# Filler matmuls in a fused attention and MoE kernel: one PSUM tile for a run of them instead of one each

## The chip, the cores and the metric

The kernel runs on one core of a Trainium2 chip. The metric is the device time of one execution in microseconds (us). Three runs of the kernel before gave 780.67, 783.67 and 1508.87 us, and their median is 783.67 us.

## The reference

Three layers follow each other. The first is an attention with a memory of 32 slots per head; its result is turned into 2304 rows of 512 numbers. The second and third are feed-forward layers on these rows. In short:

```
a      = softmax(phi, over the 32 slots)              # 4 batches, 8 heads, 576 positions
k_m    = a^T k ; v_m = a^T v                          # 32 x 64 per head
attn   = softmax(q k_m^T / 8) v_m                     # 576 x 64 per head
x      = rows of attn                                 # 2304 x 512
xn     = x / rms(x) * rms_g
h      = silu(xn @ w_gate) * (xn @ w_val)             # 2304 x 1536
x2     = h @ w_out                                    # 2304 x 512
h2     = x2 @ w_in                                    # 2304 x 2048
g      = h2 where h2 >= 1, 0 where h2 <= -1, else (h2 + 1)^2 / 4
result = g @ w_out2                                   # 2304 x 512
```

## The kernel before, in words

The kernel is one long list of instructions without loops on the chip. A planner (the class `Agenda`) runs while the program is built. Each piece of work is a stream, written as a Python generator; a stream tells the planner which engine it wants next and for how long, and the planner lets the stream with the earliest start go on. The instructions stand on each engine in the order in which the planner released them, and the engines keep that order.

The attention comes first. `soft(b)` (from line 524) takes batch b's `phi`: VectorE folds a maximum `pm` (L516), TensorE transposes it into the PSUM tile `mps` (L534), VectorE reduces it to `gm` (L539), TensorE spreads `gm` again over the partitions (L545, four matmuls), VectorE subtracts it from `phi` (L553) and ScalarE takes the exponential (L521). `memory(b)` (L603, 144 matmuls named `kvps`) then multiplies it with `k` and `v`, and L622 adds the sums. `pair(n)` makes queries (L769), scores (L720) and the attention's output (L841). Beside it the weights of the second layer come in through the buffers `raw`, are converted by ScalarE and VectorE (lines 339 to 362) and go on to the stage of `gps` and `vps` (L981). After that come `ops` (L1076), the seven products of `w_in` (L1420) and those of `w_out2` (L1543).

All loads but two are issued by SyncE's queue, in the planner's order. The first batch of loads brings `phi`, `k`, `v` of two batches and one `q`; a third `phi` follows when the first `phi`'s buffer comes free, which is after L622 of batch 0.

The change is in `heat()` (from line 578). It issues matmuls of a tile of zeros, 128x512, into a PSUM bank that nothing reads. They stand where the planner had TensorE idle, until the memory of the fourth batch is done (`HEAT`, line 40, flag `('km', 3)`). The planner books 0.2133 us for one, and picks a free bank `z` for it. Every other PSUM tile comes from the same pool, one buffer for each of the eight banks; a bank that a stream gives back is noted with its time in `agenda.given[z]`. A new tile of a pool in a buffer that an older tile held has to wait for the last user of the older tile. That wait is a semaphore on the first instruction that writes the new tile, and it is put there also where the last user was TensorE itself.

Of the kernel before, what the change touches and what calls it, by code (L numbers as in the profile page):

```python
# [9 lines left out]
F32 = mybir.dt.float32  # L10
# [6 lines left out]
P = 128  # L17
# [212 lines left out]
def tile_attn_moe(tc, q, k, v, phi, w_gate, w_val, w_out1, rms_g, w_in2, w_out2, out):  # L230
# [46 lines left out]
    psum = top.enter_context(tc.tile_pool(name="psum", bufs=1, space=bass.MemoryType.PSUM))  # L277
# [28 lines left out]
    agenda = Agenda({**BUFS, "th": 0, "xs": 0, "ab": 0, "gs": 0, "wo": 0, **{("bank", z): 1 for z in range(8)}})  # L306
# [270 lines left out]

    def heat():

        while HEAT[0] not in agenda.flags:  # L580
            z = yield "heat", 0.2133
            t = psum.tile([P, 512], F32, tag=f"b{z}", name="heat")
            nc.tensor.matmul(  # L583
                out=t.rearrange("p (x n) -> p x n", x=2), lhsT=zeros[:, 0:P],
                rhs=zeros.unsqueeze(1).to_broadcast([P, 2, 256]), start=True, stop=True,
                skip_group_check=True,
            )
# [625 lines left out]
    if HEAT:  # L1213
        add(10**6, heat())
# [451 lines left out]
```

## Time and profile before

| what | value |
|---|---|
| median of three runs | 783.67 us |
| the profiled execution | 782.0 us |
| its span | 780.2 us |
| TensorE busy in the span | 768.4 us |
| VectorE busy | 621.8 us |
| ScalarE busy | 462.9 us |
| GpSimd busy | 61.1 us |
| data moved by DMA | 197.49 MB, mean 253 GB/s |
| heat matmuls | 46, the first at 1.0 us, the last at 85.5 us |

The span runs from the first to the last instruction that the profile counts; 1.8 us of the execution lie around it. Busy time is the time in which an engine had an instruction in work; a matmul counts from its start to its modelled end, so matmuls that are pipelined overlap in it. "PE" is TensorE's matmuls, "PEld" its weight loads, DVE is VectorE, ACT ScalarE, POOL GpSimd, SP SyncE. The chain of waits is followed back from the last instruction: from each instruction to what released it, or to the one before it on its engine.

### The profile page before, as it was taken

The numbers are of one execution on the slowest core, as the hardware profiler recorded it, in microseconds if no ns is written. First come the engines' busy times: TensorE is split into PE (matmuls) and PEld (weight loads), VectorE is DVE, ScalarE is ACT, GpSimd is POOL, SyncE is SP. The second block draws the span as 40 slices with busy tenths as digits, with TensorE's granted clock in tenths as the row PEclk, the third lists the DMA queues.
The fourth block names the chain that finished last, engine by engine and source line by source line (L and its number), as shares of the span: only waits on it lengthen the run. The fifth ranks groups of instructions, "written<-read, shape, count | busy, mean of one in ns | idle before, by whom it ended". The sixth has DMA issues, their size and how long they took to land.

```text
span 780.2 us, 17231 instructions
## 1 busy us (share of the span) xinstructions
PE 768.4 (98%) x6383; PEld 701.0 (90%) x6383; DVE 621.8 (80%) x1257; ACT 462.9 (59%) x959; POOL 61.1 (8%) x84
## 2 busy tenths in 40 slices
PE   8999999999999999999999999999999999999997
PEld 1777788889989888988889999999999999999997
DVE  2798979999878787756688989997779895689963
ACT  1488877765566654656566656564457464565452
POOL 1266710000000000000000000000000000000000
PEclk9999999999999999999999999999999999999999
DMA  9984546587878765599746999779878978857876
GB/s 341 327 319 150 197 170 209 204 272 262 281 248 286 249 243 199 191 324 311 250 161 208 310 310 295 259 246 321 291 241 267 304 231 260 259 184 245 276 225 199
DMA packets 113371, 197.49 MB, mean 253 GB/s; under 512 B 10372, under 2 KB 41096, under 8 KB 113288
## 3 DMA queue, kind: packets, MB, share of 16 engines
q1 hardware_dynamic: 112368, 194.88, 75.1%
q10 hardware_dynamic: 920, 1.51, 0.5%
q8 instruction: 51, 0.84, 0.4%
q14 instruction: 32, 0.26, 0.1%
HBM read 151.26 MB, written 45.09 MB: 252 GB/s over the span
## 4 chain that ended last, share of the span: by engine, by line
PE 94%; DVE 2%; ACT 1%; issue 1%; DMA 1%; SPq 0%; DVEq 0%; ACTq 0%
PE ops L1076 18%; PE acc_b L1543 16%; PE qb L1420 12%; PE gps L981 10%; PE vps L981 10%; PE qc L1420 6%; PE acc_c L1543 6%; PE qa L1420 3%; PE vwps L931 3%; PE heat L583 3%; PE xp L841 2%; PE kvps L603 1%; PE sc L720 1%; PE qps L769 1%; DMA x1B<-x_d 1%
## 5 line engine op out<-in xcount | busy, mean ns | idle before, releaser
L1076 PE MATMUL ops<-ab,wo1h 128*128 128x512 f32 (+1 forms) x480 | 137.2, 371 | 0.5 <-ACT xs L1090 0.5
L1420 PE MATMUL qb<-xop,wr 128*128 128x384 f32 x576 | 111.9, 338 | 0.0
L1420 PEld LDWEIGHTS qb<-xop,wr 128*128 128x128 f32 x576 | 100.5, 187 | 0.9 <-DVE xop L1295 0.5
L1076 PEld LDWEIGHTS ops<-ab,wo1h 128*128 128x128 f32 x480 | 84.6, 189 | 15.8 <-issue 2.9
L1076 PE MATMUL ops<-ab,wo1l 128*128 128x512 f32 (+1 forms) x240 | 88.4, 368 | 0.0
L1543 PE MATMUL acc_b<-wor,gg_A 128*128 128x256 f32 x648 | 80.8, 280 | 1.0 <-ACT gg_A L1491 0.8
L1543 PEld LDWEIGHTS acc_b<-wor,gg_A 128*128 128x128 f32 x648 | 79.3, 188 | 1.3 <-ACT gg_A L1491 1.0
L1382 ACT ACTIVATE u<-qb 128x384 f32<-128x384 f32 x72 | 35.2, 490 | 50.0 <-PE qb L1420 49.4
L1420 PE MATMUL qc<-xop,wr 128*128 128x384 f32 x288 | 58.4, 337 | 0.0
L1543 PE MATMUL acc_c<-wor,gg_S 128*128 128x256 f32 x432 | 53.0, 279 | 0.0
L1076 PEld LDWEIGHTS ops<-ab,wo1l 128*128 128x128 f32 x240 | 45.3, 189 | 7.9
L1543 PEld LDWEIGHTS acc_c<-wor,gg_S 128*128 128x128 f32 x432 | 52.2, 188 | 0.0
L1543 PE MATMUL acc_b<-wor,gg_S 128*128 128x256 f32 x432 | 51.7, 279 | 0.0
L1543 PEld LDWEIGHTS acc_b<-wor,gg_S 128*128 128x128 f32 x432 | 51.3, 188 | 0.0
L1420 PEld LDWEIGHTS qc<-xop,wr 128*128 128x128 f32 x288 | 51.0, 187 | 0.0
L344 ACT ACTIVATE raw<-raw 128x512 uint32<-128x512 uint32 x68 | 45.4, 674 | 0.0
L1013 ACT ACTIVATE kvth<-gps 128x64 f32<-128x64 f32 (+2 forms) x101 | 28.9, 305 | 18.4 <-PE gps L981 18.2
L981 PE MATMUL gps<-late,vwh 128*128 128x288 f32 x192 | 39.6, 294 | 0.0
L981 PE MATMUL vps<-late,vwh 128*128 128x288 f32 x192 | 39.6, 294 | 0.0
L951 DVE TENSOR_TENSOR vwl<-vwps,vwh 128x512 fp32r<-128x512 f32 x48 | 32.3, 684 | 7.2 <-ACT vwh L949 6.9
L1047 ACT ACTIVATE ab<-kvth 128x512 fp32r<-128x512 f32 (+1 forms) x40 | 22.7, 567 | 24.8 <-PE ops L1076 24.8
L1491 ACT ACTIVATE gg_S<-gs 128x384 fp32r<-128x384 f32 x52 | 26.8, 522 | 17.5 <-PE acc_b L1543 8.5
(188 smaller groups left out, 1739.8 us busy)
## 6 DMA issues: line engine op xcount, KB each, us to landing
wr<-win_d SPq DMA_DIRECT2D x168, 256.0 KB, 3.9
wor<-wout_d SPq DMA_DIRECT2D x168, 256.0 KB, 3.4
raw<-in_moe_w_out_dram SPq DMA_DIRECT2D x28, 512.0 KB, 4.7
win_d<-wins SPq DMA_DIRECT2D x56, 256.0 KB, 3.3
wout_d<-wouts SPq DMA_DIRECT2D x56, 256.0 KB, 3.2
raw<-in_moe_w_in_dram SPq DMA_DIRECT2D x16, 512.0 KB, 5.1
raw<-in_moe_w_gate_dram SPq DMA_DIRECT2D x12, 512.0 KB, 4.8
raw<-in_moe_w_val_dram SPq DMA_DIRECT2D x12, 512.0 KB, 5.5
```

The lines of the kernel that those rows point to most:

```text
L344: nc.scalar.activation(out=low, in_=low, func=AF.Copy, scale=LOW_SCALE, bias=LOW_BIAS)
L583: nc.tensor.matmul(out=t.rearrange("p (x n) -> p x n", x=2), lhsT=zeros[:, 0:P], rhs=zeros.unsqueeze(1).to_broadcast([P, 2, 256]), start=T ...
L931: nc.tensor.matmul(out=vps[g][0][32 * c : 32 * c + 32, 2 * P * x : 2 * P * x + 2 * P], lhsT=vT[n // NF1 * 2 + x][hs, c, :], rhs=t[hs, c].r ...
L951: nc.vector.tensor_tensor(out=lv, in0=vps[g][0], in1=hv.bitcast(F32), op=ALU.subtract)
L981: nc.tensor.matmul(out=p[:, 0:HB], lhsT=wt[:, g, i, :], rhs=at[b][:, g, c], start=(g == 0 and y == 0), stop=(g == 1 and y == 2),)
L1013: nc.scalar.activation(out=t, in_=g[:, c], func=AF.Silu)
L1047: nc.scalar.activation(out=ah, in_=src, func=AF.Copy)
L1076: nc.tensor.matmul(out=p[:, 0:n], lhsT=wt[:, fc, d], rhs=at, start=(fc == 0 and x == 0), stop=(fc == NF1 - 1 and x == 2),)
L1382: nc.scalar.activation(out=u, in_=src, func=AF.Copy)
L1420: nc.tensor.matmul(out=bank, lhsT=wt[:, kc, :], rhs=xt[:, kc, :], start=(start and kc == 0 and i == 0), stop=(kc == 1 and i == 2), skip_gr ...
L1491: nc.scalar.activation(out=t[:, 0], in_=src, func=AF.Copy)
L1543: nc.tensor.matmul(out=acc[x + "001"[t]][:, t % 2], lhsT=g[:, gi, P * t : P * t + P], rhs=w[:, wi], start=((o, t) in FIRST and q == 0 and ...
```

## The change

A run of heat matmuls keeps its PSUM tile as long as the planner names the same bank for the next one and no stream has given that bank back in between. Otherwise it takes a new tile, as before.

```diff
     def heat():
 
+        last = t = None
         while HEAT[0] not in agenda.flags:
             z = yield "heat", 0.2133
-            t = psum.tile([P, 512], F32, tag=f"b{z}", name="heat")
+            if last != (z, agenda.given.get(z)):
+                last = z, agenda.given.get(z)
+                t = psum.tile([P, 512], F32, tag=f"b{z}", name="heat")
             nc.tensor.matmul(
```

No engine's instructions change their order, and none is added or taken away; all lines after 579 are numbered three higher. What changes are semaphore waits on TensorE: of the 46 heat matmuls, 41 lose a wait on TensorE's own semaphore, and 5 other matmuls get one.

TensorE's first instructions, before the change (`zeros` is the tile of zeros, `heat` the bank's tile, the waits stand in brackets, and a wait on TensorE itself reads PE_49):

```order
L583 LDWEIGHTS zeros [waits DVE_49]
L583 MATMUL heat<-zeros 128x512
L583 LDWEIGHTS zeros
L583 MATMUL heat<-zeros 128x512 [waits PE_49]
...
L534 MATMUL mps_174<-ident,pm_155 128x128 [waits DVE_49,Pool_49]
```

The same place in the changed program:

```order
L586 LDWEIGHTS zeros [waits DVE_49]
L586 MATMUL heat<-zeros 128x512
L586 LDWEIGHTS zeros
L586 MATMUL heat<-zeros 128x512
...
L534 MATMUL mps_155<-ident,pm_142 128x128 [waits DVE_49,Pool_49]
```

In both, 21 heat matmuls stand ahead of the transpose into `mps`; before, the second to the twenty-first wait for the one ahead of them, and after, none of them waits.

TensorE at the transpose of batch 1, before the change:

```order
L583 LDWEIGHTS zeros
L583 MATMUL heat<-zeros 128x512 [waits PE_49]
L534 MATMUL mps_322<-ident,pm_258 128x128 [waits DVE_49]
L769 MATMUL qps_0_0_324<-ident,q_203 128x128 [waits DMAHW5_49]
L769 MATMUL qps_0_0_324<-ident,q_203 128x128 x3
L657 MATMUL kT_334<-ident,kd_302 128x128
```

The same place in the changed program:

```order
L586 LDWEIGHTS zeros
L586 MATMUL heat<-zeros 128x512
L534 MATMUL mps_287<-ident,pm_229 128x128 [waits DVE_49,PE_49]
L772 MATMUL qps_0_0_289<-ident,q_176 128x128 [waits DMAHW5_49]
L772 MATMUL qps_0_0_289<-ident,q_176 128x128 x3
L660 MATMUL kT_299<-ident,kd_273 128x128
```

Here the wait has moved from the heat matmul to the transpose behind it. The other four matmuls that get such a wait are three first matmuls of a `qps` (L769 before, L772 after) and the first of an `aTp` (L820, L823).

## Rows read from the trace of the kernel before

**Rows 1.** The page: shares of the chain of waits by line.

```profile
PE ops L1076 18%; PE acc_b L1543 16%; PE qb L1420 12%; PE gps L981 10%; PE vps L981 10%; PE qc L1420 6%; PE acc_c L1543 6%; PE qa L1420 3%; PE vwps L931 3%; PE heat L583 3%; PE xp L841 2%; PE kvps L603 1%; PE sc L720 1%; PE qps L769 1%; DMA x1B<-x_d 1%
```

**Rows 2.** Stretches: us; PE, PEld, DVE, ACT, POOL busy (instructions); granted clock, DMA share, GB/s.

```profile
20.00:25.00 5.00, 4.72 (x144) 3.03 (x128) 3.37 (x16) 0.00 (x0) 0.61 (x1) 1.00 0.53 168
25.00:30.00 5.00, 4.84 (x59) 3.40 (x58) 3.02 (x5) 4.32 (x8) 1.30 (x2) 1.00 1.05 404
...
40.00:60.00 20.00, 18.58 (x387) 15.05 (x391) 18.76 (x40) 17.67 (x37) 14.08 (x16) 1.00 0.89 318
...
100.00:200.00 100.00, 100.00 (x896) 88.92 (x895) 88.60 (x191) 68.72 (x160) 2.79 (x2) 1.00 0.67 225
...
400.00:780.00 380.00, 374.32 (x2665) 372.42 (x2663) 308.83 (x601) 211.56 (x416) 0.00 (x0) 1.00 0.80 259
```

**Rows 3.** TensorE in order of time: start, us, line, operation, tiles, count.

```profile
1.04 13.41 PE L583 MATMUL heat<-zeros 128*128 128x512 bf16 x21 [1.04 <-DVE zeros L435]
14.24 0.42 PE L534 MATMUL mps<-ident,pm 128*128 128x128 f32 x1
...
16.28 3.13 PE L583 MATMUL heat<-zeros 128*128 128x512 bf16 x7
...
19.50 2.25 PE L603 MATMUL kvps<-kv,phi 64*32 64x128 f32 x144
...
22.00 2.55 PE L583 MATMUL heat<-zeros 128*128 128x512 bf16 x6
24.38 0.27 PE L534 MATMUL mps<-ident,pm 128*128 128x128 f32 x1
```

**Rows 4.** The chain of waits in order of time: start, us, what.

```profile
13.22 0.60 PE heat L583
...
16.88 0.39 PE heat L583
17.31 0.39 PE heat L583
...
44.05 1.27 issue
```

**Rows 5.** TensorE in the stage of L981, in order of time.

```profile
180.00 0.29 PE L981 MATMUL vps<-Al,vwh 128*128 128x288 f32 x1
180.13 0.29 PE L981 MATMUL vps<-Ah,vwl 128*128 128x288 f32 x1
```

**Rows 6.** VectorE in order of time: start, us, line, operation, idle ahead.

```profile
6.43 0.29 DVE L516 TENSOR_TENSOR pm<-pm,phi 128x128 f32<-128x128 f32 x1
...
16.40 1.42 DVE L553 TENSOR_TENSOR phi<-phi,mps 128x576 f32<-128x576 f32 x2 [1.41 <-PE mps L545]
...
23.29 0.28 DVE L516 TENSOR_TENSOR pm<-pm,phi 128x128 f32<-128x128 f32 x1
...
24.69 0.29 DVE L539 TENSOR_REDUCE gm<-mps 128x2 f32<-128x128 f32 x1 [0.79 <-PE mps L534]
...
25.83 1.35 DVE L553 TENSOR_TENSOR phi<-phi,mps 128x1152 f32<-128x1152 f32 x1 [0.52 <-PE mps L545]
...
42.02 1.18 DVE L341 TENSOR_SCALAR w<-raw 128x512 f32<-128x512 f32 x1
43.90 0.69 DVE L807 TENSOR_REDUCE sm<-e 128x16 f32<-128x512 f32 x1 [0.70 <-ACT e L803]
```

**Rows 7.** ScalarE in order of time: a load's issue, and the first exponential.

```profile
1.33 0.42 ACTq L465 DMA_DIRECT2D kv<-in_k_dram  x1
...
17.19 1.35 ACT L521 ACTIVATE phi<-phi 128x576 f32<-128x576 f32 x2 [10.94 <-DVE phi L553]
```

**Rows 8.** SyncE in order of time: the first gate weights' issue.

```profile
24.21 1.43 SPq L326 DMA_DIRECT2D raw<-in_moe_w_gate_dram  x1
```

**Rows 9.** Loads issued at 1.33 and at 24.21: queue, count, KB, us to landing.

```profile
kv<-in_k_dram ACTq DMA_DIRECT2D x1, 1152.0 KB, 10.0
...
raw<-in_moe_w_gate_dram SPq DMA_DIRECT2D x1, 512.0 KB, 13.3
```

## The prediction

> **What bounds the kernel now.** I read the page's chain of waits first, then stretches of the span, then each engine in order of time where the edited matmuls stand, and last the loads.
>
> The chain is TensorE nearly everywhere, and the heat matmuls, which compute nothing, are 3% of it [rows 1]. The stretches show why their place matters. From 100 us on TensorE has no gap (100.00 of 100 us; 374.32 of the last 380), so whatever brings it to 100 us earlier should end the kernel earlier by as much [rows 2]. Between 40 and 60 us TensorE (18.58 of 20), VectorE (18.76) and ScalarE (17.67) are all nearly full [rows 2].
>
> In order of time TensorE begins with 21 heat matmuls, from 1.04 to about 14.2 us, and only then comes the first real one, the transpose into `mps` at 14.24 [rows 3]. Its operand `pm` was ready on VectorE at 6.43 + 0.29 = 6.72 us [rows 6]. So the start of the kernel waits 7.5 us for filler: it has become the bound there.
>
> Why the filler is so slow shows in its records. A heat takes 0.60 us early on, and 21 of them from 1.04 to 14.45 are one per 0.64 us; from 16.88 on each takes 0.39 and starts 0.43 after the one ahead [rows 3, 4]. Each starts only when the one ahead is over, which is what a wait on TensorE itself makes. Matmuls without such a wait run closer than they last: at 180 us those of 288 columns start 0.13 apart and last 0.29, both into one bank [rows 5].
>
> **The clock.** The granted clock reads 1.00 in every stretch [rows 2], so I take the level from durations. [...] The heats of 0.60 us ran at the lower level until after 13.22, those from 16.88 on at the upper; between them stand `mps` and the heats behind it.
>
> **The change, step by step.** No instruction moves; 41 heats lose their wait and five other matmuls get one.
>
> 1. *The first 21 heats.* They now follow each other. Bounds: all at the lower level, 1.04 + 21 x 0.43 = 10.07 us; all at the upper, 1.04 + 21 x 0.22 = 5.66, but then the transpose waits for `pm`, 6.8. The clock starts low and rose in the trace once the work came closer, so I take half of them at each level: 1.04 + 10.5 x 0.43 + 10.5 x 0.22 = 7.9. Against 14.24 that is 6.4 earlier.
> 2. *From the transpose to VectorE's subtraction.* It took 16.40 - 14.24 = 2.16 us [rows 3, 6], with two waiting heats and the lower clock in it. In batch 1 the same way took 25.83 - 24.38 = 1.45, with foreign work in it, and its first leg 24.69 - 24.38 = 0.31; with `gm`'s 0.29 the least is 0.6. I take 1.2, nearer to the whole second round. The subtraction and the exponential end 17.19 + 1.35 - 16.40 = 2.14 later [rows 6, 7], unchanged. The exponential is done at 7.9 + 1.2 + 2.1 = 11.2 instead of 18.54.
> 3. *The next seven heats* delayed `kvps` to 19.50, 0.96 us after its exponential. Seven at 0.22 are 1.5 us beside 2.1 us of VectorE and ScalarE, so they vanish behind these. Now `k` is late next: issued at 1.33, landed 10.0 later, 11.33 [rows 7, 9]. `kvps` starts at about 11.4: **8.1 us earlier**. With step 1 at its slow end it would be 10.07 + 2.16 + 2.14 = 14.4, 5.1 earlier.
> 4. *Six heats at 22.00* end with the second transpose at 24.38, while its `pm` was ready at 23.29 + 0.28 = 23.57 [rows 3, 6]. Six at 0.22 are 1.3 instead of 2.55, so `pm` is what it waits for: another **0.75**.
> 5. *The other ten heats* would save up to 0.21 each, 2.1 in all. I count nothing: VectorE and ScalarE, nearly full there [rows 2], are late next. Bounds 0 to 2.1.
> 6. *Five new waits* sit on matmuls that follow heats in a bank. [...]
> 7. *What gives back: the loads.* They can't all come 8.85 us earlier. The DMA share is 0.53 from 20 to 25 us and 1.05 in the 5 us behind it [rows 2]: half of 5 us, 2.5, is empty, because the queue waits for `phi`'s buffer, and that hole closes. The first gate weights, landed at 24.21 + 13.3 = 37.5 [rows 8, 9], land at 35.0 at best. VectorE uses them at 42.02, which would now be 33.2, so it waits 1.8; 0.7 of that it idled anyway ahead of L807 [rows 6]. **Back: 1.1.** Bounds 0 (absorbed in the buffers) and the whole excess over the hole, 8.85 - 2.5 = 6.35.
>
> Sum: -8.1 - 0.75 + 1.1 = -7.75. Against the profiled execution's 782.0 us (span 780.2 and 1.8 around it) that is **774.3 us**. The median, 783.67, is 1.7 above that execution, and the nearer two of the three runs, 780.67 and 783.67, lie on both sides of it, so I use no other base.
>
> **The rivals.**
>
> *The loads become the bound.* From 25 us on the queues are full (1.05) [rows 2]. If everything up to 60 us hangs on them, only the hole's 2.5 us come through, and the end is 782.0 - 2.5 = 779.5. For it: the full queues, and three engines that are nearly full together. Against it: the gate weights landed 4.5 us ahead of their use. Anything between this and the forecast is possible too. Chance 0.25.
>
> *The change frees the wait but not the pace.* The waits are gone from the program, but if a run of writes into one bank can't come closer, nothing changes: 782. Against it stand the two matmuls in one bank at 0.13 us [rows 5]. With all other ways in which the shift could be lost before 100 us: chance 0.1.
>
> *More comes through.* The weights' delay is absorbed and the ten other heats count: 782.0 - 8.85 - 2.1 = 771.1. Chance 0.07.
>
> *Slower: the clock falls.* Shorter heats leave longer gaps ahead of `kvps` and the scores. In the trace TensorE ran at the lower level for the 13 us in which it waited after every heat [rows 3, 4]. If it falls back after the first heats and stays low to 60 us, about half of its busy time there (0.21 of the 0.39 of a heat) doubles: some 20 of its 40 us, 782.0 - 8 + 20 = 794. It becomes slower than before if it stays low for over 16 us of busy time. Against it: the same columns now stand closer together, and in the trace the clock held from 17 us on with wider spacing. [...] No row here shows a fall after 16.88, so I keep the chance at 0.06.
>
> A piece of this is already in the trace: in the middle of a batch's `kvps`, at 44.05, TensorE stood 1.27 us with nothing to wait for [rows 4]. TensorE's instructions are short there and a new block of them may have been late. With closer work one more such stop may appear, at the second `kvps`; it would raise 774.3 to 775.6. [...] I leave it in the range.
>
> **Numbers.** The forecast, a gain of 6.5 to 9 us (773 to 775.5), has 0.52; the loads' case and what lies between 0.25 (775.5 to 780); no change 0.1; more 0.07; slower 0.06. [...] The range from 772 to 780 holds the forecast, the loads' case and half of the case with more, 0.8. 2% is 15.7 us, about what a measurement of this kernel can tell from no change; nothing above gives that much, so faster by over 2% has 0.01, and slower by over 2% (over 797.7) needs the lower clock past 60 us: 0.02.
>
> **What would show it.** In the changed profile heats start 0.43 or 0.22 apart. The transpose into `mps` stands near 7.9 us (step 1), the first `kvps` near 11.4 with `k`'s load as its releaser (step 3), the second transpose at about 15.5 behind `pm` (step 4), the DMA share from 15 to 25 us has no hole, VectorE's first L341 waits for its weights near 35 (step 7), and from 100 us on TensorE is as full as before. The prediction is wrong if heats stay 0.43 or 0.64 apart at the upper clock, if records of 0.60 us reappear after 17 us, or if TensorE gets gaps of some us between 40 and 100 that give the start back.

## The result and the profile after

The changed kernel takes 773.67 us (median of six runs, 773.01 to 774.35) against 784.09 for the kernel before (median of six, one of them of 1508.87 us). The ratio of the means without that one run is 0.9881, 95% interval 0.9855 to 0.9907, a gain of 9.3 us. The other five runs of the kernel before go from 780.62 to 785.37; why they scatter so much more than those of the changed kernel stays open. The forecast was 774.3. The profiled executions' spans differ by 780.2 - 772.0 = 8.2 us, and the readings below are of these two.

TensorE in order of time, after the change (start, us, line, operation, tiles, count, idle ahead and its releaser); it answers to [rows 3, 4]:

```profile
1.04 6.04 PE L586 MATMUL heat<-zeros 128*128 128x512 bf16 x21 [1.04 <-DVE zeros L435]
6.91 0.27 PE L534 MATMUL mps<-ident,pm 128*128 128x128 f32 x1
...
7.94 1.69 PE L586 MATMUL heat<-zeros 128*128 128x512 bf16 x7
...
11.48 2.24 PE L606 MATMUL kvps<-kv,phi 64*32 64x128 f32 x144 [1.71 <-DMA kv<-in_k_dram]
...
13.97 1.47 PE L586 MATMUL heat<-zeros 128*128 128x512 bf16 x6
15.69 0.30 PE L534 MATMUL mps<-ident,pm 128*128 128x128 f32 x1 [0.25 <-DVE pm L516]
...
22.59 1.11 PE L606 MATMUL kvps<-kv,phi 64*32 64x128 f32 x61
24.55 1.50 PE L606 MATMUL kvps<-kv,phi 64*32 64x128 f32 x83 [0.85 <-issue]
25.97 0.39 PE L625 MATMUL kvps<-consts,s 64*128 64x1 f32 x4
...
34.35 1.56 PE L606 MATMUL kvps<-kv,phi 64*32 64x128 f32 x92
37.51 1.06 PE L606 MATMUL kvps<-kv,phi 64*32 64x128 f32 x52 [1.60 <-issue]
```

The 21 heats are out in 6.04 us instead of 13.41, and the first transpose starts at 6.91. The first `kvps` waits for `k`, as forecast, and starts at 11.48 instead of 19.50. The second transpose now waits 0.25 us for `pm`. New is the stop of 0.85 us inside the second `kvps` (its releaser, "issue", says that the profile shows nothing that TensorE waited for there); the one inside the third was 1.27 and is 1.60.

VectorE in order of time, against [rows 6]:

```profile
6.29 0.29 DVE L516 TENSOR_TENSOR pm<-pm,phi 128x128 f32<-128x128 f32 x1
...
8.06 1.42 DVE L553 TENSOR_TENSOR phi<-phi,mps 128x576 f32<-128x576 f32 x2 [0.54 <-PE mps L545]
...
34.64 0.43 DVE L341 TENSOR_SCALAR w<-raw 128x512 f32<-128x512 f32 x1 [0.68 <-DMA raw<-in_moe_w_gate_dram]
35.76 0.69 DVE L810 TENSOR_REDUCE sm<-e 128x16 f32<-128x512 f32 x1 [0.69 <-ACT e L806]
```

`pm` is ready at 6.58 and waits only 0.33 us for TensorE. The gate weights do hold L341, for 0.68 us, but the `sm` behind it (L810, L807 before) comes at 35.76 instead of 43.90, still 8.14 earlier. Ahead of it VectorE still idles 0.69 us for ScalarE's `e`, as before (0.70): L341 came 0.68 late but took 0.43 instead of 1.18, and `sm` waited for neither. Why L341 was shorter stays open.

The stretches, against [rows 2]; first the part where the loads had a hole:

```profile
15.00:20.00 5.00, 4.75 (x63) 3.76 (x60) 3.26 (x10) 3.49 (x7) 0.66 (x2) 1.00 1.05 393
...
40.00:60.00 20.00, 19.78 (x410) 15.56 (x409) 18.72 (x44) 16.43 (x35) 11.20 (x14) 1.00 1.03 373
...
100.00:200.00 100.00, 100.00 (x911) 88.06 (x910) 90.48 (x189) 69.06 (x156) 4.05 (x3) 1.00 0.68 230
...
400.00:772.00 372.00, 366.72 (x2607) 365.03 (x2606) 302.53 (x588) 206.56 (x405) 0.00 (x0) 1.00 0.80 259
```

The hole in the loads is gone (1.05 from 15 to 20 us, and 1.06 from 20 to 25), and from 100 us on TensorE is as full as before. One and the same group of 32 matmuls near 90 us shows how much got there, in the chain of waits of the kernel before and of the changed one:

```profile
96.81 1.02 PE vwps L931 x32
```

```profile
89.16 1.02 PE vwps L934 x32
```

7.65 us of the shift arrive there, just ahead of the part where TensorE has no gaps; the other half microsecond is made behind it, and no experiment went after it.

### The profile page after: what moved, and what is told of

Same layout as the page of the kernel before. It is cut to its first block, busy times and chain, and to the rows that moved or that the text cites. A ratio compares the mean times of both kernels' runs of the same rounds, so it can differ in the third digit from the quotient of the medians.

```text
span 772.0 us, 17234 instructions
## 1 busy us (share of the span) xinstructions
PE 759.0 (98%) x6383; PEld 700.6 (91%) x6383; DVE 621.6 (81%) x1257; ACT 462.7 (60%) x959; POOL 61.1 (8%) x84
## 4 chain that ended last, share of the span: by engine, by line
PE 92%; DVE 3%; DMA 2%; ACT 1%; issue 1%; ACTq 0%; SPq 0%; DVEq 0%
PE ops L1079 18%; PE acc_b L1546 17%; PE qb L1423 12%; PE gps L984 10%; PE vps L984 10%; PE qc L1423 6%; PE acc_c L1546 6%; PE qa L1423 3%; PE vwps L934 3%; PE xp L844 2%; DMA kv<-in_k_dram 1%; PE kvps L606 1%; PE sc L723 1%; PE qps L772 1%; DMA x1B<-x_d 1%
```

## The experiments

Two theories stood against each other. *Place:* the gain is that the first transpose no longer stands behind 21 waiting heats, up to the point where `k` lands. *Sum of waits:* each of the 41 waits costs about the same. A third question was the clock: whether dense heats help by raising it early.

**Only the first run shares a tile.**

```diff
+        n = 0
...
+            n += 1
-            if last != (z, agenda.given.get(z)):
+            if n > 21 or last != (z, agenda.given.get(z)):
```

> The first 21 heat matmuls share a tile; each of the other 25 takes a new one, so they wait for each other as before. My theory (the gain is the place of the first transpose, then k's landing): transpose near 6.9 us, first kvps still near 11.5 because seven waiting heats end near 11.0, second transpose about 0.7 later than with the whole change; time 774 to 775. Rival (each of the 41 waits is worth about the same, 0.25 us): 20 of 41 waits gone, 779 us.

Measured: 774.91 us, ratio 0.9906 (0.9874 to 0.9939). TensorE:

```profile
16.54 0.27 PE L534 MATMUL mps<-ident,pm 128*128 128x128 f32 x1
...
23.88 2.25 PE L608 MATMUL kvps<-kv,phi 64*32 64x128 f32 x144
26.06 0.39 PE L627 MATMUL kvps<-consts,s 64*128 64x1 f32 x4
```

Twenty waits carry nearly the whole gain; the equal-worth theory (779) falls. The second transpose is 0.85 us later than with the whole change, as expected, but the second `kvps` runs without a stop and its sums (26.06) come only 0.09 later than with the whole change (25.97). So in these profiles the second run of heats gains time and loses it again at that stop.

**Only the later heats share.** The condition is `n <= 22 or last != ...`.

> The first 22 heat matmuls take a new tile each, the later ones share. My theory: transpose stays near 14.2 us, first kvps comes about 1 us earlier (seven heats vanish behind the exponential), second transpose another 0.7; gain 1.5 to 2.5, time 779.5 to 781. Rival (equal worth of all waits): 779 us; rival (only the first run counts, the rest is hidden): no change, 782.

Measured: 779.47 us, ratio 0.9962 (0.9941 to 0.9983).

```profile
18.25 2.34 PE L608 MATMUL kvps<-kv,phi 64*32 64x128 f32 x144
...
22.56 0.30 PE L534 MATMUL mps<-ident,pm 128*128 128x128 f32 x1 [0.26 <-DVE pm L516]
```

The transpose stays at 14.24, the first `kvps` is 1.25 earlier and the second transpose 1.82. Alone, the later heats give some 2 us by the medians (781.38 and 779.47; 3 by the means). Together with the first run they add little: the spans of the profiles with the first run alone and with the whole change are 772.1 and 772.0, the medians 774.91 and 773.82, from two chips. `k`'s landing and the stop take their part.

**New tiles as before, but in turn over the free banks.**

```diff
+        self.heated = {}
...
-            return (at, min(free, key=lambda z: self.given.get(z, 0.0))) if free else None
+            return (at, min(free, key=lambda z: self.heated.get(z, 0))) if free else None
...
+                self.heated[z] = len(self.active) + 1
```

> Every heat matmul takes a new tile as before, but the planner gives them the free banks in turn, so that a wait on TensorE points at a heat several places back. My theory (what costs is waiting for the matmul directly ahead): heats 0.43 and 0.22 apart, time 773.5 to 775. Rival (it is the number of tiles, or of waits of any kind): 22 waits remain of 41, time 778 or more.

Measured: 774.27 us, ratio 0.9901 (0.9868 to 0.9933).

```profile
1.03 7.30 PE L585 MATMUL heat<-zeros 128*128 128x512 bf16 x21 [1.03 <-DVE zeros L437]
...
10.79 1.04 PE L585 MATMUL heat<-zeros 128*128 128x512 bf16 x4 [0.77 <-DVE phi L555]
...
11.94 2.24 PE L605 MATMUL kvps<-kv,phi 64*32 64x128 f32 x144
```

22 heats still wait on TensorE here, but for a matmul several places back, and the 21 heats come nearly as fast as with the change (7.30 us; 6.04 and, in the second profile below, 7.03). What cost was waiting for the matmul directly ahead, not the tiles or the number of waits. Taking the banks in turn has a price of its own: one heat took a bank that VectorE was still reading, waited 0.77 us for it, and the first `kvps` came at 11.94 instead of 11.48.

**The kernel before, with 12 of the first 21 heats left out.**

```diff
+            n += 1
+            if 9 < n <= 21:
+                continue
```

> The kernel before with its waits, but 12 of the first 21 heat matmuls left out. My theory (place of the transpose): nine at 0.64 us end at 6.8, transpose near 6.9 at the lower clock, exponential done near 11.2, first kvps near 11.5; time 774.5 to 776.5. Rival (the gain comes from the clock, which dense heats raise early): kvps and what follows run at the lower level for some us, kvps takes 3 us or more instead of 2.25, time 778 or more. If the stop in the second and third kvps is tied to the count of TensorE's instructions, it moves from matmul 61 and 92 of the 144 to 73 and 104.

Measured: 778.32 us, ratio 0.9949 (0.9932 to 0.9967).

```profile
6.76 0.45 PE L534 MATMUL mps<-ident,pm 128*128 128x128 f32 x1
...
8.84 4.45 PE L587 MATMUL heat<-zeros 128*128 128x512 bf16 x7
...
13.41 3.38 PE L607 MATMUL kvps<-kv,phi 64*32 64x128 f32 x144
...
26.76 1.31 PE L607 MATMUL kvps<-kv,phi 64*32 64x128 f32 x73
28.39 1.29 PE L607 MATMUL kvps<-kv,phi 64*32 64x128 f32 x71 [0.32 <-issue]
```

The transpose is where the changed kernel has it, yet most of the gain is missing: my expectation fails. At the lower clock (the transpose takes 0.45 us, 0.27 with the change) seven waiting heats take 4.45 us, so `kvps` starts at 13.41, and runs 3.38 us instead of 2.25. The run in which only the first 21 heats share a tile shows the price: it has the same waits behind the transpose, and there the transpose even stands later (7.25), but the clock is up (the transpose takes 0.27 us, the seven heats 2.99, `kvps` 2.25), and it takes 774.91, 3.4 us less on the same chip (0.32 of it by the stop in the second `kvps`, against none). Place alone is not enough; the clock is part of the gain.

**The whole change, with the same 12 heats left out.**

> The whole change, but 12 of the first 21 heat matmuls left out. If freeing the waits is what counts and the number of heats in the first run does not: transpose near 6.6, first kvps 11.5 to 11.9, time 773.5 to 775. Rival (twelve more dense heats are needed to raise the clock ahead of kvps): clock low into kvps, kvps 3 us or more, time 775.5 to 778.

Measured: 774.76 us, ratio 0.9884 (0.9858 to 0.9911). TensorE, and then stretches of 2 us with the granted clock (the third number from the end):

```profile
1.04 4.02 PE L590 MATMUL heat<-zeros 128*128 128x512 bf16 x9 [1.04 <-DVE zeros L435]
6.72 0.30 PE L534 MATMUL mps<-ident,pm 128*128 128x128 f32 x1 [1.67 <-DVE pm L516]
...
11.48 3.86 PE L610 MATMUL kvps<-kv,phi 64*32 64x128 f32 x144 [1.87 <-DMA kv<-in_k_dram]
...
24.03 1.31 PE L610 MATMUL kvps<-kv,phi 64*32 64x128 f32 x73
26.42 1.29 PE L610 MATMUL kvps<-kv,phi 64*32 64x128 f32 x71 [1.08 <-issue]
```

```profile
10.00:12.00 2.00, 0.52 (x32) 0.55 (x39) 1.74 (x5) 0.03 (x1) 0.00 (x0) 0.96 1.08 395
12.00:14.00 2.00, 2.00 (x89) 2.00 (x81) 0.69 (x1) 0.00 (x0) 0.00 (x0) 0.50 1.05 392
14.00:16.00 2.00, 2.00 (x59) 1.40 (x42) 0.27 (x3) 0.00 (x0) 0.00 (x0) 0.69 1.06 393
```

Here the fall of the clock that I had as the slower rival is seen. By their spacing the nine free heats run at the lower level (4.02 us, 0.43 apart); the transpose behind them takes 0.30, the upper level, where behind nine waiting heats it took 0.45. TensorE idles 1.67 us for `pm` ahead of the transpose and 1.87 for `k` ahead of `kvps`, and from 12 us on the granted clock is 0.50, the lower level. The first `kvps` takes 3.86 us, 1.6 more. So both expectations came half true: the time is that of the first, `kvps` that of the rival. At the end the medians are 0.9 apart (774.76 and 773.82, from one chip), but the four runs go from 773.30 to 775.45; in the two profiles the whole 1.6 is there (spans 773.4 and 771.8).

**No heats at all.** Every one is skipped.

> All 46 heat matmuls left out; they compute nothing. By what the run with nine showed (transpose at 6.8, but seven waiting heats at the lower clock put the first kvps to 13.4): the transpose near 6.7, the first kvps near 11.5, when k lands, at the lower level, 3.4 to 4.5 us long, and the lower level goes on behind it; time 775 to 780. Rival (the filler only ever delayed): as with the whole change or better, 773 to 774. Rival (without filler the clock stays low for tens of us): over 782. The stops in the second and third kvps move by 41 and 43 matmuls, to 102 and 135 of 144, if they hang on the count of instructions.

Measured: 778.34 us, where the kernel before had 784.36; ratio 0.9942 (0.9919 to 0.9965).

```profile
6.69 0.45 PE L534 MATMUL mps<-ident,pm 128*128 128x128 f32 x1 [6.69 <-DVE pm L516]
...
11.38 4.10 PE L604 MATMUL kvps<-kv,phi 64*32 64x128 f32 x144 [2.97 <-DMA kv<-in_k_dram]
...
23.93 1.73 PE L604 MATMUL kvps<-kv,phi 64*32 64x128 f32 x102
27.50 0.89 PE L604 MATMUL kvps<-kv,phi 64*32 64x128 f32 x42 [1.85 <-issue]
...
36.70 2.16 PE L604 MATMUL kvps<-kv,phi 64*32 64x128 f32 x135
40.98 0.43 PE L604 MATMUL kvps<-kv,phi 64*32 64x128 f32 x9 [2.12 <-issue]
```

With its waits the filler cost more than it brought: without any, the kernel is faster than before. Freed, the filler is worth 778.34 - 773.82 = 4.5 us. The clock is low through `kvps`, 4.10 us against 2.24, though the granted clock reads 1.00 from 12 to 16 us; here, as at the start of the two kernels' profiles (heats of 0.60 and up to 0.63 us at a granted clock of 1.00), only the durations show the lower level. Not all of the 4.5 us is shown to be the clock: the stop in the second `kvps` is a microsecond longer too (1.85 and 0.85).

**The whole change, and `k` of the first batch over two queues.**

```diff
-                    (nc.scalar if (b, i) == (0, 0) else nc.sync).dma_start(
...
+                    for c, e in ((0, nc.scalar), (2, nc.sync)) if (b, i) == (0, 0) else ((None, nc.sync),):
+                        cs = slice(0, 4) if c is None else slice(c, c + 2)
+                        e.dma_start(
...
```

> The whole change, and half of batch 0's k comes over SyncE's queue ahead of v, the other half over ScalarE's as before. My theory (k's landing at 11.3 holds the first kvps): k and v both land near 10, the first kvps starts at 10.3 to 10.6, when its exponential is done, 0.9 to 1.2 us earlier than with the change alone; of that the later loads (q of batch 0 near 15.4, the gate weights at VectorE's first L341) leave 0 to 0.8 at the end, 773.0 to 773.7. Rival (k isn't what holds kvps): kvps stays at 11.5 and the time too.

and beside it the change once more:

> The whole change once more, on the same chip as the split of k, for comparison: 773.0 to 774.4 as before. The first dense heats keep 0.43 us apart until the clock rises, and that moment differs from run to run (3.8 to 6.3 us in three profiles so far); so the transpose should lie between 6.9 and 8.2.

Measured: 773.55 us for the split (six runs, 773.13 to 773.99; ratio 0.9871, 0.9851 to 0.9892) and 773.82 for the change (six runs, 773.43 to 774.03; ratio 0.9875, 0.9852 to 0.9897). First the split, then the change:

```profile
10.94 2.33 PE L608 MATMUL kvps<-kv,phi 64*32 64x128 f32 x144 [0.87 <-DMA kv<-in_v_dram]
```

```profile
7.91 0.27 PE L534 MATMUL mps<-ident,pm 128*128 128x128 f32 x1
...
11.54 2.24 PE L606 MATMUL kvps<-kv,phi 64*32 64x128 f32 x144 [0.78 <-DMA kv<-in_k_dram]
```

`kvps` moves 0.60 forward when `k` does, less than the 0.9 to 1.2 expected, and then waits for `v`: its operands' landing is what holds it. In the second profile of the change the transpose stands a whole microsecond later than in the first (7.91, 6.91), and `kvps` at the same place: the landing hides it. The split's lead is there near 90 us too (the `vwps` of above: 88.28 with the split, 89.36 with the change), but not at the end (spans 772.2 and 771.8; the split's profiled execution is the slowest of its six):

```profile
88.28 1.02 PE vwps L936 x32
```

```profile
89.36 1.02 PE vwps L934 x32
```

Between 480 and 492 us TensorE waits for an operand of the third layer, `xop`, again first the split and then the change (who waits for whom: us, times, longest):

```profile
PE qa L1425 <- DVE xop L1300: 0.5, 1, 0.5
PE qa L1425 <- ACT xop L1298: 0.2, 1, 0.2
```

```profile
PE qa L1423 <- DVE xop L1298: 0.3, 1, 0.3
```

So in these two executions 0.4 of the lead goes into that wait; where the rest goes stays open. The two versions can't be told apart, and none tried is measurably faster than the change.

## Why the prediction was right

**Steps 1 and 2.** The 0.43 and 0.22 us from one free heat to the next, on which the 7.9, its bounds and the heats' times in steps 3 to 5 stand, were my estimate, and no row of the kernel before shows them: of its first 21 heats all but the first wait for the one ahead. The runs showed these distances: nine free heats in 4.02 us at the lower level (with 12 heats left out) are 0.43 apart, and at the upper six take 1.47 us and seven 1.69, 0.22 more. The clock rose earlier than I assumed: 6.91 - 1.04 = 5.87 us are six heats at 0.43 and fifteen at 0.22, so the transpose stood at 6.91 and not 7.9. In the second profile it stood at 7.91: the moment of the rise differs from run to run, and the forecast's half of the heats at each level lies within that scatter. The way from there to the subtraction took 8.06 - 6.91 = 1.15 (1.2 forecast).

**Step 3** is exact: `kvps` at 11.48 (11.4 forecast), with `k` as its releaser, and the split of `k` shows the cause. It also makes step 1 robust: a microsecond there is hidden.

**Steps 4 and 5.** Step 4 holds as a step, 0.67 us, since the second transpose went from 24.38 to 15.69, 8.69 earlier, and `kvps` 8.02. Step 5 (the other heats, at nothing) gave something too. The kernel before had, behind its second transpose:

```profile
31.72 2.25 PE L603 MATMUL kvps<-kv,phi 64*32 64x128 f32 x144
33.89 0.39 PE L622 MATMUL kvps<-consts,s 64*128 64x1 f32 x4
```

From the second transpose to the second `kvps` it is 31.72 - 24.38 = 7.34 us there, 23.88 - 16.54 = 7.34 with only the first run shared, and 22.59 - 15.69 = 6.90 with the whole change, so the five heats in between give 0.44. What the other five give was not taken apart. Neither gain stayed. From the start of the second `kvps` to its sums it was 2.17 us and is 3.38, with the stop of 0.85 in it, and the sums come 33.89 - 25.97 = 7.92 earlier, no more than the first `kvps`. I had named that stop and left it in the range; the sum should have had it as a term that takes back step 4. With only the first run shared the stop was absent, and 0.85 us of the second transpose cost 0.09 behind `kvps`.

**Step 6** (the new waits, not in the sum): the second transpose waits 0.25 us for `pm`, not for its heats, as its releaser shows.

**Step 7** was too large: the gate weights were late by 0.68, and the `sm` behind them did not wait for it; I had booked 1.1. So one term of +1.1 and one of -0.75 were both near 0 in the end, and they nearly cancelled.

**Luck.** That the sum of -7.75 met the 7.65 us near 90 us so closely owes something to these two errors. It also starts from one execution of 782.0 us of a kernel that scatters from 780.62 to 785.37, and by the means the gain is 9.3. The prediction took 2% for about what a measurement of this kernel can tell from no change; the interval came out at some 0.3% to either side.

**The rivals.** The loads as the bound (779.5) fell: the queues are full to 60 us, 1.03, and the shift came through. The case with more (771.1) did not come, since the stop took what steps 4 and 5 gave. The unchanged pace fell with the heats' spacing, 0.22 us, and the run over banks in turn shows that the wait on the matmul ahead set it. The clock's fall did not happen in the changed kernel, but it is real: with 12 heats fewer it happened, and its price was 1.6 us in `kvps`, not the 20 that I had made of it up to 60 us from the 0.21 between a heat of 0.60 and one of 0.39. The granted clock was 0.50 from 12 to 14 us, 0.69 from 14 to 16 and 1.00 from 16 to 18, with TensorE busy in 2.00 us of each of the first two stretches.

## What to carry to other kernels

A filler that a planner books at its streaming time has to be able to stream: look whether each one waits for the one ahead, which shows as a start just after the other's end (0.60 us long and one per 0.64 here), and whether the first real instruction behind it was ready long before. Freed filler is worth keeping: with 12 heats fewer the first `kvps` took 3.86 us and with none 4.10, instead of 2.24, so leave out none before looking at the durations of the matmuls in the stretch that it covers, and not only at the granted clock, which read 1.00 where durations showed the lower level. Price the next bound before counting a gain; here `k`'s landing hid whether the first run ended at 6.9 or at 7.9 us.

## What the runs showed of the hardware

**TensorE stopped inside a row of equal matmuls, at a count of instructions.** With the change the stop lies at matmul 61 of 144 in the second `kvps` and at 92 in the third. With 12 heats (24 instructions, each matmul with its weight load) fewer it lies at 73 in the second, in both kernels that left them out; with the 41 heats that stand ahead left out, at 102, and in the third, 43 heats ahead, at 135. So it hangs on the place in the program. In the changed kernel a third, shorter stop follows:

```profile
43.91 0.71 PE L734 MATMUL sc<-kmT,qr 64*64 64x32 f32 x17 [0.22 <-issue]
```

By the count of the rows 253 matmuls lie between its first and second stop and 127 between the second and the third, with their weight loads 506 and 254 instructions. A stop's length seems to hang on how fast TensorE gets through the instructions ahead of it: in the second `kvps` none before the change and none with only the first run shared, 0.32 with nine heats and their waits, 0.85 with the change, 1.08 with nine free heats, 1.85 with none. The longest is 2.12 us (the third `kvps` without heats). The pages of both kernels have a DMA queue of instructions (packets, MB, share of the 16 engines' span):

```profile
q8 instruction: 51, 0.84, 0.4%
```

If it is TensorE's, its 6383 matmuls and 6383 weight loads are some 250 instructions to a packet, by my estimate. The distances, 506 and 254, are close to two packets and one; that TensorE waits for such a packet at a stop, the new block of the prediction, is not shown.

**The clock rose at a moment that differed from run to run.** The same 21 dense heats took 6.04 and 7.03 us in two profiles of one program (the transpose at 6.91 and 7.91), and 7.30 with banks in turn. That is 0.99 us between two executions of one program; here the landing of `k` hides it (`kvps` at 11.48 and 11.54).
